# Word transposes of the probabilities, alternating with the score matmuls, in a two-problem attention kernel

## The chip, the cores and the metric

The kernel runs on one core of one Trainium2 chip. The metric is the time of one execution on the device in microseconds (us). Each figure for "the time" is the median of several executions. A profile of one further execution gives the starts and durations of the instructions on each engine: PE (TensorE matmuls; PEld is its weight load), DVE (VectorE), ACT (ScalarE), POOL (GpSimd) and SP (SyncE, which here only issues transfers).

## The reference

Two independent attention blocks, A and B, of the same sizes; their outputs stand side by side in the last dimension. In each, queries are projected from `x`, keys and values come from caches, and there is one softmax over 512 keys:

```python
B, Sq, D = 16, 144, 448
H, Sk, Dh = 16, 512, 256
q = (x @ wq).reshape(B, Sq, H, Dh).transpose(0, 2, 1, 3)
scores = jnp.einsum("bhqd,bhkd->bhqk", q, k_cache) * (Dh ** -0.5)
p = softmax(scores, axis=-1)
o = jnp.einsum("bhqk,bhkd->bhqd", p, v_cache)
out = o.transpose(0, 2, 1, 3).reshape(B, Sq, H * Dh) @ wo
...
return jnp.concatenate([a, b], axis=-1)
```

All inputs and outputs are bf16. Block B repeats its key heads by `Hq // Hkv`, which is 1.

## The kernel before

**Units.** A unit is one (block, batch, head): 2 x 16 x 16 = 512 units `U`. Four units make a group (one load of values, `t_load_v`, 1 MB), eight make a supergroup (one transposing load of keys, `t_load_k`). Of the 144 queries of a unit, the first 112 (`QA`) are worked on alone, and the last 32 (`QB`) of four units are put together into 128 rows. The first kind is called the 112-row part here, the second the 32-row part.

**The stages of a unit**, each with its engine:

- `t_q` (PE, L314): eight matmuls of 144 columns project the queries into the PSUM bank `qp_ps`; `t_evac_q` copies them to `qt_sb`, on DVE (L326) in four of eight iterations and on ACT (L330) in the others.
- `t_sa` (PE, L418): two matmuls of 512 columns, one for each half of the head's 256 dimensions, accumulate the scores of the 112-row part into one of two banks `sa_ps`, chosen by the unit's parity.
- `t_max` (DVE, L429), `t_exp` (ACT, L440, an activation and a read of its row sums), `t_recip` (DVE, L450) and `t_norm` (POOL, L458): the softmax. The probabilities stand in `pa_sb`, keys in the free dimension.
- `t_ta` (PE, L471): four transposes bring the keys to the partitions. Transpose `c` takes every fourth key, beginning at key `c`, so that partition `p` holds keys 4p to 4p+3, as the values are laid out. The result goes to the bf16 view `pta_ps` of the same bank `sa_ps`, chosen by parity again; `t_evac_pta` (DVE, L481) copies it to `pt_sb`.
- `t_pv` (PE, L504): eight matmuls of 144 columns with the values as weights, moving operand `pt_sb`; `t_evac_ot` (ACT, L519) copies the result to `ring`.
- `t_op_piece` (PE, L542): matmuls of 448 columns with `wo`, usually two for each iteration; more or none where chunks come due.

The 32-row part has the same stages for four units at once in the banks `sb_ps`: `t_sb` (L342, 16 matmuls for eight units), `t_max_b` (L354), `t_exp_b` (L364), `t_recip_b` (L374), `t_norm_b` (L382), `t_tb` (L394, four transposes of 128 columns) and `t_evac_ptb` (L403).

**Order.** One loop over `i` writes every engine's instruction list in program order. Iteration `i` handles Q of unit i+15 (`LQ`), scores, max and exp of unit i+5 (`LS`), reciprocal and normalisation of unit i+4, transposes of unit i+2 (`LT`) with their copy, and PV and its evacuation of unit i. On PE the order in an iteration is Q, SB (every eighth), SA, TA, TB (two in eight), PV, output matmuls. The queue SP issues the loads in an order planned by due times.

**Waits.** The class `_Sched` turns reads, writes and banks into semaphore waits, one wait for each engine, put ahead of the first instruction of an entry. An entry counts its engine's semaphore once, after its last instruction. The PSUM bank is a resource: an entry that touches a bank waits for the last use of that bank by another engine. Iteration `i` puts the scores of unit i+5 into one `sa_ps` bank; iteration i+1 puts the transposes of unit i+3 into the same bank, and iteration i+2 the scores of unit i+7. So each bank goes from scores (read by max and exp) to transposes (read by the copy) to scores again.

Of the kernel before, what the change touches and what calls it, by code (L numbers as in the profile page):

```python
# [5 lines left out]
BF16 = mybir.dt.bfloat16  # L6
F32 = mybir.dt.float32
# [115 lines left out]
def bass_concat_heads__mha_block_cached__gqa_block_cached__near_ridge_kernel(  # L123
# [19 lines left out]
    Bn, SQ, D = A_x.shape  # L143
    H, SK, DH = A_k_cache.shape[1], A_k_cache.shape[2], A_k_cache.shape[3]
    assert (SQ, D, SK, DH) == (144, 448, 512, 256), (SQ, D, SK, DH)
    assert H % 4 == 0
    QA, QB = 112, 32
    NU = Bn * H
    NT = NP * NU
# [11 lines left out]
    LQ, LS, LT = 15, 5, 2  # L161
# [3 lines left out]
    NQT, NPA, NPB, NPT, NST, NSTB, NOST = 12, 5, 2, 8, 4, 2, 3  # L165
# [9 lines left out]
    with contextlib.ExitStack() as es:  # L175
        def sb(name, shape, dt):
            return es.enter_context(nc.sbuf_tensor(name, shape, dt))

        def ps(name, shape, dt):
            return es.enter_context(nc.psum_tensor(name, shape, dt))  # L180
# [4 lines left out]
        kt_sb = sb("kt_sb", [128, NK, 2, 8 * SK], BF16)  # L185
        v_sb = sb("v_sb", [128, NV, 4, 4 * DH], BF16)
        xt_sb = sb("xt_sb", [128, NXG, 4, XB * SQ], BF16)
        qt_sb = sb("qt_sb", [128, NQT, 2, SQ], BF16)
        pa_sb = sb("pa_sb", [128, NPA, SK], BF16)
        pb_sb = sb("pb_sb", [128, NPB, SK], BF16)  # L190
        pt_sb = sb("pt_sb", [128, NPT, 4, SQ], BF16)
        ost_sb = sb("ost_sb", [128, NOST, D], BF16)
        ident = sb("ident", [128, 128], BF16)
        ones = sb("ones", [128, 128], BF16)
        stat = sb("stat", [128, 3 * NST + 3 * NSTB + 2], F32)
        qp_ps = ps("qp_ps", [128, 512], F32)
        sa_ps = [ps("sa_ps%d" % i, [128, 512], F32) for i in range(2)]
        sb_ps = [ps("sb_ps%d" % i, [128, 512], F32) for i in range(2)]
        ot_ps = [ps("ot_ps%d" % i, [128, 512], F32) for i in range(2)]
        op_ps = ps("op_ps", [128, 512], F32)  # L200
        pta_ps = [t.bitcast(BF16) for t in sa_ps]
        ptb_ps = [t.bitcast(BF16) for t in sb_ps]

        S = _Sched()
        sem_names = list(COMPUTE)
# [127 lines left out]
        def t_sb(SG):  # L333
            ksl = SG % NK

            def e(t):
                ins = None
                for dc in range(2):
                    for jj in range(8):
                        U = 8 * SG + jj  # L340
                        j = jj % 4
                        ins = t.matmul(sb_ps[jj // 4][32 * j:32 * j + 32, :], lhsT=qt_sb[:, U % NQT, dc, QA:SQ],  # L342
                                       rhs=kt_sb[:, ksl, dc, jj * SK:(jj + 1) * SK], start=(dc == 0), stop=(dc == 1),
                                       tile_position=(0, 32 * j))
                return ins
            S.add(PE, e, reads=[(("qt", (8 * SG + jj) % NQT), 8 * SG + jj) for jj in range(8)] + [(("kt", ksl), SG)],
                  writes=[(("sbb", 0), ("s", 2 * SG)), (("sbb", 1), ("s", 2 * SG + 1))], banks=["sb0", "sb1"],
                  name="SB%d" % SG)
# [38 lines left out]
        def t_tb(G):  # L387
            psl = G % NPB

            def e(t):  # L390
                src = pb_sb[:, psl, :].rearrange("q (p c) -> q c p", c=4)
                ins = None
                for c in range(4):
                    ins = t.transpose(ptb_ps[G % 2][:, c * 128:(c + 1) * 128], src[:, c, :], ident[:, :])  # L394
                return ins
            S.add(PE, e, reads=[(("pb", psl), (G, 1)), ("ident", 0)], writes=[(("sbb", G % 2), ("t", G))],
                  banks=["sb%d" % (G % 2)], name="TB%d" % G)

        def t_evac_ptb(G):
            s0 = (4 * G) % NPT  # L400

            def e(v):
                return v.tensor_copy(pt_sb[:, s0:s0 + 4, :, QA:SQ],  # L403
                                     ptb_ps[G % 2][:, 0:512].rearrange("p (c j q) -> p j c q", c=4, j=4))
            S.add(DVE, e, reads=[(("sbb", G % 2), ("t", G))],
                  writes=[(("ptb", (4 * G + j) % NPT), 4 * G + j) for j in range(4)], banks=["sb%d" % (G % 2)],
                  name="eptb%d" % G)

        def t_sa(U):
            SG = U // 8  # L410
            ksl = SG % NK
            bank = U % 2
            ko = (U % 8) * SK

            def e(t):
                ins = None
                for dc in range(2):
                    ins = t.matmul(sa_ps[bank][0:QA, :], lhsT=qt_sb[:, U % NQT, dc, 0:QA],  # L418
                                   rhs=kt_sb[:, ksl, dc, ko:ko + SK], start=(dc == 0), stop=(dc == 1))
                return ins  # L420
            S.add(PE, e, reads=[(("qt", U % NQT), U), (("kt", ksl), SG)], writes=[(("sap", bank), ("s", U))],
                  banks=["sa%d" % bank], name="SA%d" % U)

        def t_max(U):
            bank = U % 2
            sl = U % NST

            def e(v):
                return v.tensor_reduce(stat[0:QA, NEG + sl:NEG + sl + 1], sa_ps[bank][0:QA, :], axis=AX.X,  # L429
                                       op=ALU.max, negate=True)  # L430
            S.add(DVE, e, reads=[(("sap", bank), ("s", U))], writes=[(("neg", sl), U)], banks=["sa%d" % bank],
                  name="mx%d" % U)

        def t_exp(U):
            bank = U % 2
            sl = U % NST
            psl = U % NPA

            def e(a):
                return a.activation(pa_sb[0:QA, psl, :], sa_ps[bank][0:QA, :], AF.Exp,  # L440
                                    bias=stat[0:QA, NEG + sl:NEG + sl + 1], scale=1.0,
                                    accum_out=stat[0:QA, RSUM + sl:RSUM + sl + 1])
            S.add(ACT, e, reads=[(("sap", bank), ("s", U)), (("neg", sl), U)],
                  writes=[(("pa", psl), (U, 0)), (("rsum", sl), U)], banks=["sa%d" % bank], name="ex%d" % U)
# [15 lines left out]
            S.add(POOL, e, reads=[(("pa", psl), (U, 0)), (("rinv", sl), U)], writes=[(("pa", psl), (U, 1))],  # L460
                  name="nm%d" % U)

        def t_ta(U):
            psl = U % NPA
            bank = U % 2

            def e(t):
                src = pa_sb[0:QA, psl, :].rearrange("q (p c) -> q c p", c=4)
                ins = None
                for c in range(4):  # L470
                    ins = t.transpose(pta_ps[bank][:, c * 128:c * 128 + QA], src[:, c, :], ident[0:QA, 0:QA])  # L471
                return ins
            S.add(PE, e, reads=[(("pa", psl), (U, 1)), ("ident", 0)], writes=[(("sap", bank), ("t", U))],
                  banks=["sa%d" % bank], name="TA%d" % U)

        def t_evac_pta(U):
            sl = U % NPT
            bank = U % 2

            def e(v):  # L480
                return v.tensor_copy(pt_sb[:, sl, :, 0:QA],  # L481
                                     pta_ps[bank][:, 0:512].rearrange("p (c q) -> p c q", c=4)[:, :, 0:QA])
            S.add(DVE, e, reads=[(("sap", bank), ("t", U))], writes=[(("pta", sl), U)], banks=["sa%d" % bank],
                  name="epta%d" % U)

# [8 lines left out]
        def t_pv(U):  # L494
            G, j = divmod(U, 4)
            vsl = G % NV
            sl = U % NPT
            ob = U % 2

            def e(t):  # L500
                ins = None
                for dc in range(2):
                    for c in range(4):
                        ins = t.matmul(ot_ps[ob][:, dc * SQ:(dc + 1) * SQ],  # L504
                                       lhsT=v_sb[:, vsl, j, c * DH + dc * 128:c * DH + (dc + 1) * 128],
                                       rhs=pt_sb[:, sl, c, :], start=(c == 0), stop=(c == 3))
                return ins
            S.add(PE, e, reads=[(("v", vsl), G), (("pta", sl), U), (("ptb", sl), U)], writes=[(("otp", ob), U)],
                  banks=["ot%d" % ob], name="PV%d" % U)
# [75 lines left out]
        for XG in range(NXGT):  # L585
            pr, j = divmod(XG, Bn // XB)
# [64 lines left out]
        i = s_min  # L651
        while True:
# [21 lines left out]
            u = i + LQ  # L674
# [2 lines left out]
                t_evac_q(u)  # L677
            if do_sb and sgi > 0:
                t_sb(sgi)
            u = i + LS  # L680
            if 0 <= u < NT:
                t_sa(u)
                t_max(u)
                t_exp(u)
            u = i + LS - 1
            if 0 <= u < NT:
                t_recip(u)
                t_norm(u)
            u = i + LT
            if 0 <= u < NT:  # L690
                t_ta(u)
                t_evac_pta(u)
            if ok and ph == 3:
                t_tb(ga)
                t_evac_ptb(ga)
# [7 lines left out]
            u = i  # L703
# [97 lines left out]
```

## Time and profile before

| what | us |
|---|---|
| time, median of three runs (1212.93 to 1215.47) | 1213.23 |
| span of the profiled execution, first to last instruction | 1210.9 |
| PE busy with Q, L314, 4096 matmuls of 0.228 | 344.1 |
| PE busy with PV, L504, 4096 matmuls of 0.226 | 340.9 |
| PE busy with scores, L418, 1024 matmuls of 0.385 | 311.1 |
| PE busy with output matmuls, L542, 1120 of 0.353 | 279.6 |
| PE busy with transposes, L471, 2048 of 0.213 | 186.5 |

The span is 2.3 us under the median; the time also has what lies around the first and last instruction. Matmuls of PE overlap: the next one starts while the last drains, so a matmul's duration is longer than its share of the time, and the times in the table add up to more than the span. What a matmul costs in a row of matmuls is read from the distance between starts. The granted TensorE clock of the profiled execution was 0.997 of full speed.

In a line of the page's table of groups stand the code line, the engine, the operation, the tiles (out<-in), shapes and count; then, after the first bar, the time in which the group was busy and the mean duration of one instruction in ns; after the second, how long the engine was idle just before them and who ended most of that idle time. A line of the timeline has the start (us from the start of the span), the duration of the whole run of like instructions, the engine and line, the shapes, and in brackets the idle time before it with its releaser. A line of the tile view has the shortest, median and longest duration in ns.

### The profile page before, as it was taken

What the parts mean: (1) busy time and instruction counts of PE and PEld (TensorE: products, weight loads), DVE (VectorE), ACT (ScalarE), POOL (GpSimd) and SP (SyncE); (2) the same over time, 40 slices, a digit from 0 to 9 for tenths busy, and PEclk for the clock granted to TensorE, in tenths of its full rate; (3) what the DMA queues carried; (4) which work ended last, traced back from release to release, by engine and by line L of the source; (5) the groups of instructions that cost most, each with busy time, mean ns of one, the idle gap of its engine ahead of it and who ended that gap; (6) DMA issues with size and microseconds to landing.
All of it is one profiled execution on the core that took longest, in us unless ns stands there. A gap on an engine that the chain in (4) does not pass through costs nothing.

```text
span 1210.9 us, 33868 instructions
## 1 busy us (share of the span) xinstructions
PE 1176.6 (97%) x13952; PEld 902.6 (75%) x13952; DVE 770.1 (64%) x2179; ACT 753.9 (62%) x2213; POOL 679.6 (56%) x682
## 2 busy tenths in 40 slices
PE   4998999999999999999999999999999999999997
PEld 3676777777777777777777777777877777777765
DVE  1765666666666666666566666666666666666563
ACT  1655666666666666666566666666666666666553
POOL 0654565565555565565555655655655655655553
PEclk9999999999999999999999999999999999999999
DMA  9999999999999999999999999999999999999971
GB/s 250 296 269 290 246 255 225 242 251 246 245 238 234 228 263 231 239 239 233 278 284 272 278 272 267 247 257 224 245 245 236 226 245 244 244 239 243 223 178 47
DMA packets 627033, 294.15 MB, mean 243 GB/s; under 512 B 548416, under 2 KB 556608, under 8 KB 626880
## 3 DMA queue, kind: packets, MB, share of 16 engines
q1 hardware_dynamic: 625152, 287.85, 102.2%
q0 software_dynamic: 1728, 4.13, 1.2%
q8 instruction: 111, 1.82, 0.6%
q14 instruction: 42, 0.34, 0.1%
HBM read 148.90 MB, written 4.13 MB: 126 GB/s over the span
## 4 chain that ended last, share of the span: by engine, by line
PE 90%; DMA 6%; DVE 2%; SPq 1%; ACT 0%; issue 0%; POOL 0%; ACTq 0%
PE qp_ps L314 20%; PE ot_ps L504 19%; PE sa_ps L418 18%; PE op_ps L542 17%; PE sa_ps L471 8%; PE sb_ps L342 5%; DMA kt_sb<-in_A_k_cache_dram 4%; PE sb_ps L394 2%; DMA kt_sb<-in_B_k_cache_dram 1%; DVE stat L429 1%; DMA wq_sb<-in_A_wq_dram 0%; PE qp_ps L542 0%; SPq L280 0%; DVE qt_sb L326 0%; DVE pt_sb L481 0%
## 5 line engine op out<-in xcount | busy, mean ns | idle before, releaser
L458 POOL TENSOR_TENSOR pa_sb<-pa_sb,stat 112x512 bf16<-112x512 bf16 x512 | 532.7, 1041 | 491.6 <-DVE stat L450 491.4
L440 ACT ACTIVATE pa_sb<-sa_ps,stat 112x512 bf16<-112x512 f32 x512 | 352.0, 688 | 409.6 <-DVE stat L429 408.6
L429 DVE TENSOR_REDUCE stat<-sa_ps 112x1 f32<-112x512 f32 x512 | 353.9, 691 | 324.7 <-PE sa_ps L418 321.4
L314 PEld LDWEIGHTS qp_ps<-xt_sb,wq_sb 128*128 128x128 bf16 x4096 | 290.5, 99 | 93.1 <-issue 11.3
L314 PE MATMUL qp_ps<-xt_sb,wq_sb 128*128 128x144 bf16 x4096 | 344.1, 228 | 16.1 <-DMA wq_sb<-in_A_wq_dram 10.3
L504 PE MATMUL ot_ps<-pt_sb,v_sb 128*128 128x144 bf16 x4096 | 340.9, 226 | 0.0
L418 PE MATMUL sa_ps<-kt_sb,qt_sb 128*112 128x512 bf16 x1024 | 311.1, 385 | 1.0 <-DVE pt_sb L481 0.8
L542 PE MATMUL op_ps<-wo_sb,ring 128*128 128x448 bf16 x1120 | 279.6, 353 | 0.0
L504 PEld LDWEIGHTS ot_ps<-pt_sb,v_sb 128*128 128x128 bf16 x4096 | 269.1, 98 | 0.4
L471 PEld LDWEIGHTS sa_ps<-ident,pa_sb 112*128 112x128 bf16 x2048 | 161.2, 114 | 104.9 <-ACT pa_sb L440 24.8
L519 ACT ACTIVATE ring<-ot_ps 128x288 bf16<-128x288 f32 (+8 forms) x512 | 190.3, 372 | 4.5 <-PE ot_ps L504 4.5
L481 DVE COPY pt_sb<-sa_ps 128x448 bf16<-128x448 bf16 x512 | 190.5, 372 | 2.4 <-PE sa_ps L471 2.4
L471 PE MATMUL sa_ps<-ident,pa_sb 112*128 112x112 bf16 x2048 | 186.5, 213 | 0.1
L326 DVE TENSOR_SCALAR qt_sb<-qp_ps 128x288 bf16<-128x288 f32 x256 | 117.0, 457 | 98.2 <-PE qp_ps L314 97.5
L382 POOL TENSOR_TENSOR pb_sb<-pb_sb,stat 128x512 bf16<-128x512 bf16 x128 | 133.1, 1040 | 27.1 <-DVE stat L374 27.1
L330 ACT ACTIVATE qt_sb<-qp_ps 128x288 bf16<-128x288 f32 x256 | 106.0, 414 | 35.1 <-PE qp_ps L314 33.4
L418 PEld LDWEIGHTS sa_ps<-kt_sb,qt_sb 128*112 128x112 bf16 x1024 | 96.9, 129 | 38.5 <-issue 26.8
L542 PEld LDWEIGHTS op_ps<-wo_sb,ring 128*128 128x128 bf16 x1120 | 95.5, 98 | 28.1 <-issue 0.9
L440 ACT ACTIVATION_READ_ACCUMULATOR pa_sb<-sa_ps,stat 112x1 f32 x512 | 98.9, 193 | 0.0
L354 DVE TENSOR_REDUCE stat<-sb_ps 128x1 f32<-128x512 f32 x128 | 87.1, 680 | 3.6 <-PE sb_ps L342 3.6
L364 ACT ACTIVATE pb_sb<-sb_ps,stat 128x512 bf16<-128x512 f32 x128 | 88.5, 691 | 0.0
L450 DVE RECIPROCAL stat<-stat 112x1 f32<-112x1 f32 x512 | 78.4, 153 | 0.5 <-ACT pa_sb L440 0.5
(23 smaller groups left out, 368.4 us busy)
## 6 DMA issues: line engine op xcount, KB each, us to landing
v_sb<-in_A_v_cache_dram SPq DMA_DIRECT2D x64, 1024.0 KB, 6.0
v_sb<-in_B_v_cache_dram SPq DMA_DIRECT2D x64, 1024.0 KB, 6.1
out_dram<-ost_sb POOLq DMA_DIRECT2D x36, 112.0 KB, 5.1
wo_sb<-in_A_wo_dram SPq DMA_DIRECT2D x8, 448.0 KB, 7.4
wo_sb<-in_B_wo_dram SPq DMA_DIRECT2D x8, 448.0 KB, 5.7
wq_sb<-in_A_wq_dram SPq DMA_DIRECT2D x4, 768.0 KB, 6.2
wq_sb<-in_B_wq_dram SPq DMA_DIRECT2D x4, 768.0 KB, 7.8
wq_sb<-in_A_wq_dram SPq DMA_DIRECT2D x4, 128.0 KB, 6.6
```

Source lines behind the costliest of these rows:

```text
L314: ins = t.matmul(qp_ps[:, dc * SQ:(dc + 1) * SQ], lhsT=wq_sb[:, kc, c0:c0 + 128], rhs=xt_sb[:, xsl, kc, xo:xo + SQ], start=(kc == 0 and dc ...
L326: return v.tensor_scalar(qt_sb[:, sl, :, :], src, 1.0 / 16.0, None, op0=ALU.mult)
L382: return g.tensor_tensor(pb_sb[:, psl, :], pb_sb[:, psl, :], stat[:, RINVB + sl:RINVB + sl + 1].to_broadcast([128, SK]), op=ALU.mult)
L418: ins = t.matmul(sa_ps[bank][0:QA, :], lhsT=qt_sb[:, U % NQT, dc, 0:QA], rhs=kt_sb[:, ksl, dc, ko:ko + SK], start=(dc == 0), stop=(dc == 1))
L429: return v.tensor_reduce(stat[0:QA, NEG + sl:NEG + sl + 1], sa_ps[bank][0:QA, :], axis=AX.X, op=ALU.max, negate=True)
L440: return a.activation(pa_sb[0:QA, psl, :], sa_ps[bank][0:QA, :], AF.Exp, bias=stat[0:QA, NEG + sl:NEG + sl + 1], scale=1.0, accum_out=stat ...
L458: return g.tensor_tensor(pa_sb[0:QA, psl, :], pa_sb[0:QA, psl, :], stat[0:QA, RINV + sl:RINV + sl + 1].to_broadcast([QA, SK]), op=ALU.mult)
L471: ins = t.transpose(pta_ps[bank][:, c * 128:c * 128 + QA], src[:, c, :], ident[0:QA, 0:QA])
L481: return v.tensor_copy(pt_sb[:, sl, :, 0:QA], pta_ps[bank][:, 0:512].rearrange("p (c q) -> p c q", c=4)[:, :, 0:QA])
L504: ins = t.matmul(ot_ps[ob][:, dc * SQ:(dc + 1) * SQ], lhsT=v_sb[:, vsl, j, c * DH + dc * 128:c * DH + (dc + 1) * 128], rhs=pt_sb[:, sl, c, ...
L519: ins = a.activation(ring[:, 2 * h:2 * h + 2, c0:c0 + n1], src[:, :, 0:n1], AF.Copy)
L542: ins = t.matmul(acc[0:m, 0:D], lhsT=ring[:, c, col0:col0 + m], rhs=wo_sb[:, c, :], start=(c == first), stop=(c == last))
```

## The change

A probability is 2 bytes; two neighbouring keys make a 4-byte word. After the change the transposes move words: `pa_sb` and `pb_sb` are viewed as F32 (`pa_w`, `pb_w`), a transpose `c` takes every second word, and two transposes bring over what four did. The identity is F32. `pt_sb` keeps the two keys of a word side by side for each query, so PV's moving operand takes every second bf16 element. The copies go from bf16 views (`pta_h`, `ptb_h`) of the banks to `pt_sb`.

The entries `t_sa` and `t_ta` become one entry for each matmul and each transpose, and the loop writes them alternately: first score matmul of unit i+5, first transpose of unit i+2, second score matmul, second transpose. The max and the exp of unit i+5 are written after these; the order on DVE, ACT, POOL and SP stays as it was. In the 32-row part the two word transposes stand together, in the old place.

```diff
-        pt_sb = sb("pt_sb", [128, NPT, 4, SQ], BF16)
+        pt_sb = sb("pt_sb", [128, NPT, 2, SQ, 2], BF16)
...
-        ident = sb("ident", [128, 128], BF16)
-        ones = sb("ones", [128, 128], BF16)
+        ident = sb("ident", [128, 128], F32)
+        ones = sb("ones", [128, 128], F32)
...
-        pta_ps = [t.bitcast(BF16) for t in sa_ps]
-        ptb_ps = [t.bitcast(BF16) for t in sb_ps]
+        pta_ps = sa_ps
+        ptb_ps = sb_ps
+        pta_h = [t.bitcast(BF16) for t in sa_ps]
+        ptb_h = [t.bitcast(BF16) for t in sb_ps]
+        pa_w = pa_sb.bitcast(F32)
+        pb_w = pb_sb.bitcast(F32)
...
-                src = pb_sb[:, psl, :].rearrange("q (p c) -> q c p", c=4)
+                src = pb_w[:, psl, :].rearrange("q (p c) -> q c p", c=2)
                 ins = None
-                for c in range(4):
+                for c in range(2):
                     ins = t.transpose(ptb_ps[G % 2][:, c * 128:(c + 1) * 128], src[:, c, :], ident[:, :])
...
-                return v.tensor_copy(pt_sb[:, s0:s0 + 4, :, QA:SQ],
-                                     ptb_ps[G % 2][:, 0:512].rearrange("p (c j q) -> p j c q", c=4, j=4))
+                return v.tensor_copy(pt_sb[:, s0:s0 + 4, :, QA:SQ, :].rearrange("p j c q e -> p j c (q e)"),
+                                     ptb_h[G % 2][:, 0:512].rearrange("p (c j q) -> p j c q", c=2, j=4))
...
-        def t_sa(U):
+        def t_sa(U, dc):
...
-                ins = None
-                for dc in range(2):
-                    ins = t.matmul(sa_ps[bank][0:QA, :], lhsT=qt_sb[:, U % NQT, dc, 0:QA],
-                                   rhs=kt_sb[:, ksl, dc, ko:ko + SK], start=(dc == 0), stop=(dc == 1))
-                return ins
+                return t.matmul(sa_ps[bank][0:QA, :], lhsT=qt_sb[:, U % NQT, dc, 0:QA],
+                                rhs=kt_sb[:, ksl, dc, ko:ko + SK], start=(dc == 0), stop=(dc == 1))
...
-        def t_ta(U):
+        def t_ta(U, c):
...
-                src = pa_sb[0:QA, psl, :].rearrange("q (p c) -> q c p", c=4)
-                ins = None
-                for c in range(4):
-                    ins = t.transpose(pta_ps[bank][:, c * 128:c * 128 + QA], src[:, c, :], ident[0:QA, 0:QA])
-                return ins
+                src = pa_w[0:QA, psl, :].rearrange("q (p c) -> q c p", c=2)
+                return t.transpose(pta_ps[bank][:, c * 128:c * 128 + QA], src[:, c, :], ident[0:QA, 0:QA])
...
-                return v.tensor_copy(pt_sb[:, sl, :, 0:QA],
-                                     pta_ps[bank][:, 0:512].rearrange("p (c q) -> p c q", c=4)[:, :, 0:QA])
+                return v.tensor_copy(pt_sb[:, sl, :, 0:QA, :].rearrange("p c q e -> p c (q e)"),
+                                     pta_h[bank][:, 0:512].rearrange("p (c q) -> p c q", c=2)[:, :, 0:2 * QA])
...
-                                       rhs=pt_sb[:, sl, c, :], start=(c == 0), stop=(c == 3))
+                                       rhs=pt_sb[:, sl, c // 2, :, c % 2], start=(c == 0), stop=(c == 3))
...
-            u = i + LS
-            if 0 <= u < NT:
-                t_sa(u)
-                t_max(u)
-                t_exp(u)
+            us, ut = i + LS, i + LT
+            for half in range(2):
+                if 0 <= us < NT:
+                    t_sa(us, half)
+                if 0 <= ut < NT:
+                    t_ta(ut, half)
+            if 0 <= us < NT:
+                t_max(us)
+                t_exp(us)
...
-            u = i + LT
-            if 0 <= u < NT:
-                t_ta(u)
-                t_evac_pta(u)
+            if 0 <= ut < NT:
+                t_evac_pta(ut)
```

In the prediction SA.0, SA.1, TA.0 and TA.1 are the first and second score matmul and the first and second transpose of an iteration.

More of the change, by code (lines that the diff above doesn't have):

```diff
@@ L415, in e @@
             def e(t):
-                ins = None
-                for dc in range(2):
-                    ins = t.matmul(sa_ps[bank][0:QA, :], lhsT=qt_sb[:, U % NQT, dc, 0:QA],
-                                   rhs=kt_sb[:, ksl, dc, ko:ko + SK], start=(dc == 0), stop=(dc == 1))
-                return ins
+                return t.matmul(sa_ps[bank][0:QA, :], lhsT=qt_sb[:, U % NQT, dc, 0:QA],
+                                rhs=kt_sb[:, ksl, dc, ko:ko + SK], start=(dc == 0), stop=(dc == 1))
             S.add(PE, e, reads=[(("qt", U % NQT), U), (("kt", ksl), SG)], writes=[(("sap", bank), ("s", U))],
-                  banks=["sa%d" % bank], name="SA%d" % U)
+                  banks=["sa%d" % bank], name="SA%d.%d" % (U, dc))
         def t_max(U):
@@ L467, in e @@
             def e(t):
-                src = pa_sb[0:QA, psl, :].rearrange("q (p c) -> q c p", c=4)
-                ins = None
-                for c in range(4):
-                    ins = t.transpose(pta_ps[bank][:, c * 128:c * 128 + QA], src[:, c, :], ident[0:QA, 0:QA])
-                return ins
+                src = pa_w[0:QA, psl, :].rearrange("q (p c) -> q c p", c=2)
+                return t.transpose(pta_ps[bank][:, c * 128:c * 128 + QA], src[:, c, :], ident[0:QA, 0:QA])
             S.add(PE, e, reads=[(("pa", psl), (U, 1)), ("ident", 0)], writes=[(("sap", bank), ("t", U))],
-                  banks=["sa%d" % bank], name="TA%d" % U)
+                  banks=["sa%d" % bank], name="TA%d.%d" % (U, c))
         def t_evac_pta(U):
```

## The prediction

> **What bounds the kernel now.** I read the page's busy times first, then the waits, then the timeline of single units (a unit is one batch and head). Times are us where no unit stands. The page:
>
> ```profile
> span 1210.9 us, 33868 instructions
> PE 1176.6 (97%) x13952; PEld 902.6 (75%) x13952; DVE 770.1 (64%) x2179; ACT 753.9 (62%) x2213; POOL 679.6 (56%) x682
> ...
> L440 ACT ACTIVATE pa_sb<-sa_ps,stat 112x512 bf16<-112x512 f32 x512 | 352.0, 688 | 409.6 <-DVE stat L429 408.6
> L429 DVE TENSOR_REDUCE stat<-sa_ps 112x1 f32<-112x512 f32 x512 | 353.9, 691 | 324.7 <-PE sa_ps L418 321.4
> ...
> L504 PEld LDWEIGHTS ot_ps<-pt_sb,v_sb 128*128 128x128 bf16 x4096 | 269.1, 98 | 0.4
> L471 PEld LDWEIGHTS sa_ps<-ident,pa_sb 112*128 112x128 bf16 x2048 | 161.2, 114 | 104.9 <-ACT pa_sb L440 24.8
> ```
>
> PE is the bound, so shorter PE work ought to pay. But PE waits inside a unit must be checked first. This is the timeline of an ordinary unit:
>
> ```profile
> 601.56 0.59 PE L418 MATMUL sa_ps<-kt_sb,qt_sb 128*112 128x512 bf16 x2
> ...
> 602.00 0.36 PE L471 MATMUL sa_ps<-ident,pa_sb 112*128 112x112 bf16 x4
> ...
> 602.19 0.67 PE L504 MATMUL ot_ps<-pt_sb,v_sb 128*128 128x144 bf16 x8
> 602.20 0.69 DVE L429 TENSOR_REDUCE stat<-sa_ps 112x1 f32<-112x512 f32 x1
> ...
> 602.70 0.54 PE L542 MATMUL op_ps<-wo_sb,ring 128*128 128x448 bf16 x2
> ...
> 602.92 0.69 ACT L440 ACTIVATE pa_sb<-sa_ps,stat 112x512 bf16<-112x512 f32 x1 [0.93 <-DVE stat L429]
> ...
> 603.07 0.66 PE L314 MATMUL qp_ps<-xt_sb,wq_sb 128*128 128x144 bf16 x8
> 603.51 0.19 ACT L440 ACTIVATION_READ_ACCUMULATOR pa_sb<-sa_ps,stat 112x1 f32 x1
> ...
> 603.57 0.59 PE L418 MATMUL sa_ps<-kt_sb,qt_sb 128*112 128x512 bf16 x2
> ```
>
> Differences of starts give the stream times: two scores 0.43, four transposes 0.19 (0.047 each, 112 columns), PV 0.51, two output matmuls 0.37, Q 0.50; the unit takes 2.01. Read the softmax beside it: the max ends 602.89, exp and its accumulator end 603.70, just before the next transposes. Those write the bank that this exp reads (banks alternate by unit parity: scores of i+5, then transposes of i+3). So the transposes of one iteration wait for the exp of the iteration before. A stretch without output matmuls shows that wait ending last:
>
> ```profile
> 324.18 0.69 DVE L429 TENSOR_REDUCE stat<-sa_ps 112x1 f32<-112x512 f32 x1
> ...
> 325.29 0.64 PE L418 MATMUL sa_ps<-kt_sb,qt_sb 128*112 128x512 bf16 x2
> ...
> 325.50 0.19 ACT L440 ACTIVATION_READ_ACCUMULATOR pa_sb<-sa_ps,stat 112x1 f32 x1
> ...
> 325.74 0.24 PEld L471 LDWEIGHTS sa_ps<-ident,pa_sb 112*128 112x128 bf16 x4 [0.28 <-ACT pa_sb L440]
> ```
>
> The weight load starts 0.05 after the accumulator read ends (325.69). The max starts 0.04 after the second score matmul's record (0.38) ends: 325.29+0.64=325.93 against 325.96. So from the start of the second score matmul to the release of the next iteration's transposes: 0.38+0.04+1.51 (324.18 to 325.69)+0.05=1.98; finer starts over 84 such places give **1.972**.
>
> **The change part by part.**
>
> *Fewer transposes.* Two per unit instead of four and, at L394, two instead of four per four units. If a word streams like a bf16 key, a unit saves 2x0.047=0.094 and each of 128 TBs about 0.10 of its 0.22. The trace has no 4-byte matmul. Bounds: 0.047 each (nearest row, L471, same columns), or four times that, 0.19. I take 0.047; the half-speed and four-fold cases are rivals.
>
> The Trainium skill speaks on both sides: "FP8 and Floating Point Precision", TensorE Precision Notes, gives true FP32 four passes; "TensorE: Matmul & The Clock Gate", Terms, calls transpose mode four times faster for FP32. No row here decides; by the first rule the sum would be that of the four-fold rival, by the second that of my value.
>
> *Weight loads.* These rows of the tile view give the price by columns:
>
> ```profile
> L342 PEld LDWEIGHTS sb_ps<-kt_sb,qt_sb x1024: 92/97/151, 23.7 to 1170.3; 128*32 128x32 bf16 x171
> L418 PEld LDWEIGHTS sa_ps<-kt_sb,qt_sb x1024: 126/130/130, 28.8 to 1194.3; 128*112 128x112 bf16 x171
> ```
>
> 80 more columns cost 33 ns, 0.41 each. A 128-column load escapes this at L504 (98 ns). For words I take the slow rate, 128x0.41=0.053 exposed where nothing covers it, bounds 0.026 (the spacing of L471's first two loads where they had waited) and 0.107 (twice 0.053). In the new order each word load has a 0.21 score matmul before it as cover, except where its wait ends last.
>
> *The new order.* SA.0, TA.0, SA.1, TA.1. Nothing on DVE, ACT, POOL or SP is reordered, but TA.0 carries the wait for the previous iteration's exp, and SA.1 is now queued behind it on PE. DVE's max waits for SA.1, the exp for the max, the next TA.0 for the exp: a loop of **one** iteration, whereas before both scores went ahead of the wait. A unit's interval cannot be under 1.972 + word load 0.053 + TA.0 0.047 + what remains of SA.1's load (112 columns, 0.046, under a 0.047 stream: 0 to 0.05, I take 0.02) = **2.09**, bounds 2.05 and 2.15. An ordinary unit's PE work alone would fall to 1.92. So TA.0 would wait: from SA.1's start PE reaches TA.0 after 0.21+0.05+0.51+0.37+0.50+0.21=1.85, but the release comes at 1.972. What is late next is SA.1, with it the max; the loop keeps it so.
>
> The 511 intervals between successive second score matmuls, by starts in the timeline: 72 of mean 1.77 (no output matmul), 17 of 1.906, 224 of 2.012, 45 of 2.237 (nearly all with a TB), 153 of mean 2.97 (score blocks of the 32-row part, more output matmuls, DMA waits). With floor 2.09:
> 72x0.32=+23.0; 17x0.184=+3.1; 224x0.078=+17.5; 45x(2.09-2.237)=-6.6; 153x-0.094=-14.4; TB in 64 of the long ones, -0.10 each=-6.4. Sum **+16.2**. Each 0.01 of floor is worth 313 to 355 intervals, about 3.4 us; the balance lies at 2.045.
>
> *Other edits.* At two iterations in eight L354's max (0.68) follows the copy on DVE and L326's evacuation (0.46) comes next, ahead of the loop's max: 1.47+0.68+0.46=2.61 after SA.1's start against 2.09+0.42=2.51 wanted. Bounds 0 and 128x0.10=13; I take +5. Copies L481 (0.37) and L403 move the same bytes in longer runs: 0; L481's own loop, 0.42+0.68+0.37+0.06+0.05+0.21+0.05=1.84, is covered by 2.09. The identity in f32 is two POOL instructions at the start, under the first 10.3 us wait for wq: 0, or under 1 if uncovered. PV now reads pt_sb at a step of two. L471's load at a step of four takes 114 against 98 at L504, so bounds 0 and 15 ns x8=0.12 per unit; short units cover it (2.09-1.92=0.17), the 153 long ones would pay 18. I take 0, as moving rows here run at column rate. No DMA issue moves; V loads on SP wait for PE already (235 us behind L542), so they follow. The places where PE waits for kt_sb (7.9+0.8 us) absorb part of what is lost ahead of them: 0 to -9, I take -4.
>
> *Sum.* +16+5-4=+17 on the profiled span 1210.9, which is 2.3 below the 1213.23 median of the runs; with the same 2.3 around it, **1230**. Own range: floor 2.05 to 2.15 (+2 to +37), DVE 0 to 13, PV 0 to 18, absorption to -9, TB gain absent +11 (most of it under the floor): 1214 to 1262.
>
> **Rivals.**
>
> *Faster: the exp is not what TA.0 waits for.* Then PE streams: 512x0.094+128x0.10=61 less, of which some 11 stay with the short units held by L481's loop at 1.84: 1163. For: PE busy 97%, the waits view charges only 24.8 us to this exp, DVE and ACT are under 65% busy. Against: the load in the ordinary unit starts only 0.04 after the release (603.79 against 603.70+0.05). It decides from a floor below 2.045, which needs load, stream and remainder within 0.07; at a floor of 2.00 it gives 1199.
>
> *Half speed.* Word loads 0.107, streams 0.094: no stream gained, floor 1.972+0.107+0.094=2.17. 72x0.40+17x0.26+224x0.16=69, less 45x0.07=3: about +66, 1279. For: twice the bytes per column. Against: no row shows bytes, rather than columns, set the pace.
>
> *Four-fold.* Each word transpose 0.19: a unit +0.19, TB +0.21, floor 1.972+0.053+0.19=2.215: 72x0.45+17x0.31+224x0.20+45x0.40+153x0.19+64x0.21=+143, 1356, and up to 1410 if each pass loads again.
>
> **How the numbers follow.** Forecast 0.56; half speed 0.14; four-fold 0.13; faster 0.12; balance within 0.2% 0.05 (0.2%, 2.4 us, is about what this kernel's runs can tell from no change). The likeliest's time is 1230. The range runs from 1198, which takes in a floor of 2.00 and some two fifths of the faster case, to 1300, above half speed: left out are 0.13 above and 0.07 below. Faster 0.12, same 0.05, slower 0.83.
>
> **What would show it.** In the timeline after: a load of L471 (its new line) idle before it with the exp as releaser in most units; ordinary intervals at 2.07 to 2.13 instead of 2.01, and the 1.78 ones gone; ACT's wait for L429 and PE idle time up, DVE and ACT busy sums unchanged. Wrong if ordinary intervals are near 1.92 (no loop), if two word transposes take more than 0.12 where nothing waits (speed), or if PV's eight take over 0.51.

## The result, and the profile after

The change makes the kernel **slower**: 1284.72 us median of four runs (1284.00 to 1285.32) against 1214.29 (1212.93 to 1215.47) of the kernel before on the same chip; ratio 1.058, interval 1.0564 to 1.0596. The profiled span went from 1210.9 to 1282.3, 71.4 more. The forecast was slower, by 17: the direction was right, and the loss is four times the one forecast. The granted clock of the profiled execution was 0.999, against 0.997 before, so the loss is not the clock's. Times are in us below where no unit stands.

The page after, with the lines that answer to those of before:

```profile
span 1282.3 us, 31308 instructions
PE 1248.4 (97%) x12672; PEld 987.7 (77%) x12672; DVE 775.4 (60%) x2179; ACT 748.7 (58%) x2213; POOL 679.3 (53%) x682
...
L441 ACT ACTIVATE pa_sb<-sa_ps,stat 112x512 bf16<-112x512 f32 x512 | 351.8, 687 | 488.9 <-DVE stat L430 488.7
L430 DVE TENSOR_REDUCE stat<-sa_ps 112x1 f32<-112x512 f32 x512 | 354.2, 692 | 404.6 <-PE sa_ps L420 402.6
...
L470 PE MATMUL sa_ps<-ident,pa_sb 112*128 112x112 f32 x1024 | 300.8, 294 | 2.6 <-ACT pa_sb L441 0.2
...
L470 PEld LDWEIGHTS sa_ps<-ident,pa_sb 112*128 112x128 f32 x1024 | 202.6, 198 | 72.4 <-ACT pa_sb L441 71.9
```

DVE and ACT do the same work for as long as before (ACT's exp 351.8 against 352.0), but each waits 80 longer: ACT for the max, the max for the scores. PE has 1024 transposes in the 112-row part instead of 2048 and still shows 97% busy; "busy" includes matmuls whose record is open while the next instruction waits (below, the first score matmul is on record from 645.16 to 645.54, while the load after it waits until 645.43). So PE's idle time, which the prediction wanted up, stayed at 34. The last line names the wait: the loads of the word transposes stood 71.9 behind the exp, against 24.8 before. One such load takes 198 ns on average, against 114.

Two stretches of the timeline show it. First an iteration in which nothing waits for the exp, then, 2 us later, one in which the first transpose does:

```profile
643.36 0.26 PE L470 MATMUL sa_ps<-ident,pa_sb 112*128 112x112 f32 x1
...
643.46 0.38 PE L420 MATMUL sa_ps<-kt_sb,qt_sb 128*112 128x512 bf16 x1
...
643.67 0.26 PE L470 MATMUL sa_ps<-ident,pa_sb 112*128 112x112 f32 x1
...
643.77 0.68 PE L502 MATMUL ot_ps<-pt_sb,v_sb 128*128 128x144 bf16 x8
643.87 0.69 DVE L430 TENSOR_REDUCE stat<-sa_ps 112x1 f32<-112x512 f32 x1 [4.47 <-PE sa_ps L420]
...
644.60 0.69 ACT L441 ACTIVATE pa_sb<-sa_ps,stat 112x512 bf16<-112x512 f32 x1 [4.42 <-DVE stat L430]
...
645.16 0.38 PE L420 MATMUL sa_ps<-kt_sb,qt_sb 128*112 128x512 bf16 x1
645.18 0.19 ACT L441 ACTIVATION_READ_ACCUMULATOR pa_sb<-sa_ps,stat 112x1 f32 x1
...
645.43 0.19 PEld L470 LDWEIGHTS sa_ps<-ident,pa_sb 112*128 112x128 f32 x1 [0.19 <-ACT pa_sb L441]
...
645.64 0.38 PE L420 MATMUL sa_ps<-kt_sb,qt_sb 128*112 128x512 bf16 x1
```

In the first, a word transpose holds PE for 0.10 (643.36 to 643.46 and 643.67 to 643.77): two words cost 0.20, what four bf16 transposes cost. In the second, the accumulator read ends at 645.37, the load starts 0.06 later, and only 0.21 after that the second score matmul starts. The whole chain stands in these lines: second score matmul (643.46), max (643.87), exp (644.60), accumulator read (645.18), load of the next iteration's first transpose (645.43), which is 1.97 in all, and then that iteration's second score matmul (645.64). In 356 of 509 iterations the load starts within 60 ns of the accumulator read's end, against 87 before.

The starts of the second score matmul give an interval for each unit. Sorted by what each interval was before:

| interval before, count, mean | mean after | sum of differences |
|---|---|---|
| under 1.85, 72, 1.770 | 2.164 | +28.4 |
| 1.85 to 1.99, 17, 1.906 | 2.186 | +4.8 |
| 1.99 to 2.13, 224, 2.012 | 2.184 | +38.7 |
| 2.13 to 2.30, 45, 2.237 | 2.281 | +2.0 |
| over 2.30, 153, 2.969 | 2.953 | -2.5 |

Unrounded, the sum is 71.3, all but 0.1 of the difference of the spans. 311 of the 511 intervals are 2.18 or 2.19 after the change: a floor, not a spread.

### The profile page after: what moved, and what is told of

Same layout as the page of the kernel before. It is cut to its first block, busy times and chain, and to the rows that moved or that the text cites. A ratio compares the mean times of both kernels' runs of the same rounds, so it can differ in the third digit from the quotient of the medians.

```text
span 1282.3 us, 31308 instructions
## 1 busy us (share of the span) xinstructions
PE 1248.4 (97%) x12672; PEld 987.7 (77%) x12672; DVE 775.4 (60%) x2179; ACT 748.7 (58%) x2213; POOL 679.3 (53%) x682
## 4 chain that ended last, share of the span: by engine, by line
PE 94%; DVE 2%; DMA 2%; issue 1%; SPq 0%; ACT 0%; POOL 0%; ACTq 0%
PE ot_ps L502 20%; PE qp_ps L318 19%; PE sa_ps L420 19%; PE op_ps L540 16%; PE sa_ps L470 12%; PE sb_ps L346 5%; PE sb_ps L398 2%; DMA kt_sb<-in_B_k_cache_dram 2%; DVE stat L430 1%; DMA wq_sb<-in_A_wq_dram 0%; DVE pt_sb L407 0%; DVE pt_sb L479 0%; PE qp_ps L540 0%; DVE qt_sb L330 0%; ACT qt_sb L334 0%
## 5 line engine op out<-in xcount | busy, mean ns | idle before, releaser
L441 ACT ACTIVATE pa_sb<-sa_ps,stat 112x512 bf16<-112x512 f32 x512 | 351.8, 687 | 488.9 <-DVE stat L430 488.7
L420 PE MATMUL sa_ps<-kt_sb,qt_sb 128*112 128x512 bf16 x1024 | 381.9, 386 | 2.8 <-DVE pt_sb L479 1.1
L502 PE MATMUL ot_ps<-pt_sb,v_sb 128*128 128x144 bf16 x4096 | 348.4, 226 | 0.0
L502 PEld LDWEIGHTS ot_ps<-pt_sb,v_sb 128*128 128x128 bf16 x4096 | 300.2, 97 | 10.6
L470 PE MATMUL sa_ps<-ident,pa_sb 112*128 112x112 f32 x1024 | 300.8, 294 | 2.6 <-ACT pa_sb L441 0.2
L470 PEld LDWEIGHTS sa_ps<-ident,pa_sb 112*128 112x128 f32 x1024 | 202.6, 198 | 72.4 <-ACT pa_sb L441 71.9
L420 PEld LDWEIGHTS sa_ps<-kt_sb,qt_sb 128*112 128x112 bf16 x1024 | 167.9, 164 | 48.7 <-issue 26.8
```

The lines of the kernel that those rows point to most:

```text
L420: return t.matmul(sa_ps[bank][0:QA, :], lhsT=qt_sb[:, U % NQT, dc, 0:QA], rhs=kt_sb[:, ksl, dc, ko:ko + SK], start=(dc == 0), stop=(dc == 1))
L470: return t.transpose(pta_ps[bank][:, c * 128:c * 128 + QA], src[:, c, :], ident[0:QA, 0:QA])
L502: ins = t.matmul(ot_ps[ob][:, dc * SQ:(dc + 1) * SQ], lhsT=v_sb[:, vsl, j, c * DH + dc * 128:c * DH + (dc + 1) * 128], rhs=pt_sb[:, sl, c ...
```

## The experiments

All ratios are to the kernel before on the same chip.

**Words in the old order.** Only the loop is put back:

```diff
             for half in range(2):
                 if 0 <= us < NT:
                     t_sa(us, half)
+            for half in range(2):
                 if 0 <= ut < NT:
                     t_ta(ut, half)
```

> The words stay, the order goes back: both score matmuls, then both word transposes. Loop theory (the loss comes from TA.0's wait for the exp standing ahead of SA.1): the 2.18 us floor goes; ordinary intervals between second score matmuls 2.03 to 2.05 (2.01 before, plus 0.017 for the pair of words and 0.017 for PV's strided operand), short ones 1.78 again, time 1225 to 1236. Rival (the words themselves cost it, as loads and streams at half speed on PE, in any order): about as after the change, 1275 to 1290, ordinary intervals over 2.15.

Measured 1231.14, ratio 1.0143 (1.0128 to 1.0158). The timeline of an ordinary unit:

```profile
656.20 0.59 PE L420 MATMUL sa_ps<-kt_sb,qt_sb 128*112 128x512 bf16 x2
...
656.42 0.41 PEld L470 LDWEIGHTS sa_ps<-ident,pa_sb 112*128 112x128 f32 x2
...
656.63 0.38 PE L470 MATMUL sa_ps<-ident,pa_sb 112*128 112x112 f32 x2
...
656.85 0.36 PE L502 MATMUL ot_ps<-pt_sb,v_sb 128*128 128x144 bf16 x3
```

And the line of the waits view for the transposes' loads (total, times, longest):

```profile
PEld sa_ps L470 <- ACT pa_sb L441: 23.3, 87, 0.5
```

In the timeline the loads have no bracket, so they do not wait, and in the whole run their wait for the exp is back at what it was before (23.3 against 24.8); the two words take 0.22 (656.63 to 656.85) against 0.19 to 0.20 for four bf16 transposes. 221 intervals are 2.04 or 2.05 and 69 are 1.78 again; the floor is gone. So 17 of the 70 lost come with the words in the old order (PV's strided reading and the split entries included), and 53 only with the new order.

**The order alone, with bf16 transposes.** The kernel before, with `t_sa` and `t_ta` cut in two and written alternately, two transposes ahead of the second score matmul or one:

```diff
-                t_sa(u)
...
-                t_ta(u)
...
+            us, ut = i + LS, i + LT
+            for half, cs in enumerate((range(0, 2), range(2, 4))):
+                if 0 <= us < NT:
+                    t_sa(us, half)
+                if 0 <= ut < NT:
+                    t_ta(ut, cs)
```

(In the other run `range(0, 1), range(1, 4)`.)

> The kernel before with the order alone changed: first score matmul, two bf16 transposes, second score matmul, two bf16 transposes. Loop theory: floor 1.972 + first load 0.03 + two streams about 0.10 = 2.10, 313 intervals lifted to it, time 1250 to 1265. Rival (words cost it): 1211 to 1217.

> As the run with two transposes first, but one transpose ahead of the second score matmul and three behind. Loop theory: floor lower by one stream, 2.05, time 1236 to 1250, some 16 us under the run with two first. Rival (words cost it): 1211 to 1217, no difference between the two.

Measured 1252.98, ratio 1.0331 (1.0314 to 1.0348) with two first, and 1239.35, ratio 1.0213 (1.0197 to 1.0228) with one first. Both are as expected; between them lie 13.6, where some 16 were expected. The instructions are those of the kernel before; only PE's order differs, and the entries are split, as they also are in the run with words in the old order, where that and the words together cost 17. From the waits view and the timeline of the run with two first, then from the timeline of the run with one first:

```profile
PEld sa_ps L468 <- ACT pa_sb L437: 75.3, 312, 0.7
```

```profile
652.76 0.19 ACT L437 ACTIVATION_READ_ACCUMULATOR pa_sb<-sa_ps,stat 112x1 f32 x1
...
653.01 0.15 PEld L468 LDWEIGHTS sa_ps<-ident,pa_sb 112*128 112x128 bf16 x2 [0.20 <-ACT pa_sb L437]
...
653.14 0.38 PE L416 MATMUL sa_ps<-kt_sb,qt_sb 128*112 128x512 bf16 x1
```

```profile
651.74 0.19 ACT L437 ACTIVATION_READ_ACCUMULATOR pa_sb<-sa_ps,stat 112x1 f32 x1
...
651.99 0.11 PEld L468 LDWEIGHTS sa_ps<-ident,pa_sb 112*128 112x128 bf16 x1 [0.16 <-ACT pa_sb L437]
...
652.07 0.38 PE L416 MATMUL sa_ps<-kt_sb,qt_sb 128*112 128x512 bf16 x1
```

The same wait, as often (312 times) as after the change. What differs is the distance from the load's start to the second score matmul: 0.131 with two transposes (653.01 to 653.14), 0.082 with one (651.99 to 652.07), 0.211 with one word. The interval of the units that are held follows it: 2.104, 2.055 and 2.185 (medians). In all three the rest is **1.973** within 0.001, the time from a second score matmul through max and exp to the start of the next first load. So whatever stands between the release and the second score matmul is paid once in each unit that is held. The rival (order without effect) is out.

**Words from neighbouring places.** Each word transpose of the 112-row part takes 128 neighbouring words instead of every second one. Probabilities then meet other keys' values, and the 112-row part's output differs.

```diff
-                src = pa_w[0:QA, psl, :].rearrange("q (p c) -> q c p", c=2)
+                src = pa_w[0:QA, psl, :].rearrange("q (c p) -> q c p", c=2)
```

> As after the change, but the two word transposes of the 112-row part take 128 neighbouring words each instead of every second one, so probabilities meet other keys' values and that part of the output differs. Tells why the word load takes 195 ns: if by the 4-byte width, loads stay at 195 ns, floor 2.18, time 1282 to 1288. If by the step of two words, loads fall to some 140 ns, floor 2.13, time 1255 to 1270.

Measured 1268.87, ratio 1.0457 (1.0441 to 1.0472). The tile view, shortest, median and longest in ns; first after the change, then this run:

```profile
L470 PEld LDWEIGHTS sa_ps<-ident,pa_sb x1024: 194/196/224, 33.8 to 1270.8; 112*128 112x128 f32 x171
L470 PE MATMUL sa_ps<-ident,pa_sb x1024: 259/261/375, 33.8 to 1270.9; 112*128 112x112 f32 x171
```

```profile
L470 PEld LDWEIGHTS sa_ps<-ident,pa_sb x1024: 137/142/272, 34.1 to 1255.5; 112*128 112x128 f32 x171
L470 PE MATMUL sa_ps<-ident,pa_sb x1024: 257/261/394, 34.1 to 1255.6; 112*128 112x112 f32 x171
```

The load falls from 196 to 142, so the step of two words costs it 54 ns. The 142 lie close to the 137 that the bf16 loads of 32 and 112 columns (97 and 130) would give at 128, if they went on at the same rate. But the bf16 loads that do have 128 columns are shorter: 98 from neighbouring places (PV before) and 113 at a step of four (the transposes before). So against the load that it replaces the word load is 83 longer, 54 of it by its own step; the other 29 came with the change from bf16 at a step of four to neighbouring words, and no run takes these apart further. The floor falls by about as much as the load, to 2.127, with 0.155 from load to score matmul. The transpose itself is as long as before, so its 0.100 is not the step's doing.

**Two things in the kernel before.** The table of intervals showed 72 short ones, most of 1.78, where PE has only 1.63 of work (no output matmuls: 2.01-0.38). In the kernel before, 72 intervals are of 1.80 or less. Three runs try to win that back without the change: the reciprocal written after the transposes' copy; the output matmuls spread out; both.

```diff
-            u = i + LS - 1
-            if 0 <= u < NT:
-                t_recip(u)
-                t_norm(u)
...
                 t_evac_pta(u)
+            u = i + LS - 1
+            if 0 <= u < NT:
+                t_recip(u)
+                t_norm(u)
...
-                credit += OP_RATE
+                credit += 2.0 if len(fifo["op"]) <= 40 else 2.5
+            if i < u_tail0 - 14:
+                credit = min(credit, 3.0)
```

> The kernel before with one thing moved on DVE: the reciprocal of unit i+4 (and its normalisation on POOL) is written after the copy of the transposes instead of ahead of it. If the 72 short intervals of 1.78 are held by DVE's chain max, reciprocal, copy to the next score matmul, they fall to some 1.71 and the time by 4 to 6, to about 1209. Rival (short intervals are held by something else, or the later normalisation holds the transposes back): 1212 to 1217 or more.

> The kernel before with the output matmuls spread more evenly: two in an iteration, four now and then, instead of ten at once and then iterations without any. If an interval without output matmuls loses 0.15 to DVE's chain, some 50 of these fewer give 6 to 9 less, 1205 to 1208. Rival (PE's total work sets the time, wherever the output matmuls stand): 1212 to 1216.

> Both together. If both act on the same intervals, the sum is less than the parts: some 1204 to 1207. Rival: 1212 to 1217.

| kernel | median | ratio, interval | intervals of 1.80 or less |
|---|---|---|---|
| reciprocal after copy | 1212.91 | 0.9979 (0.9967 to 0.9990) | 71, most now 1.72 |
| spread out | 1209.29 | 0.9948 (0.9932 to 0.9964) | 42, most 1.78 |
| both | 1208.79 | 0.9946 (0.9930 to 0.9962) | 42, most 1.72 |

The reciprocal: the short intervals fell by 0.06 as the DVE chain asks, 3.6 in the profile, but the long intervals of that execution gave 3.0 back, most at places that are long before too (1.2 and 1.5 early, 3.4 at the change from A to B); which wait ends last there stays open. Of the 4 to 6 expected, some 2 came out, and the time lies in the rival's range, although the short intervals did fall. Spreading: 5.6 of the expected 6 to 9, with 30 short intervals fewer instead of 50. Neither this nor both together reached the time expected (1205 to 1208 and 1204 to 1207). Both together differ from spreading alone by less than the intervals. These two are the best versions seen, half a per cent under the kernel before.

## Why the prediction was right and wrong

**Right: the loop.** The forecast said that TA.0 would wait for the previous iteration's exp, with SA.1 queued behind it, and that this makes a floor of 1.972 plus what lies between release and SA.1. The first part has a median of 1.973 or 1.974 in all four kernels with the new order (after the change, the two with bf16, the one with neighbouring words), and the order alone, without words, loses 3.3%. That ordinary intervals would be one even number and the 1.78 ones gone came true.

**Wrong: the size of two terms in that sum.** The step that failed is "If a word streams like a bf16 key", with "I take 0.047", and beside it "For words I take the slow rate, 128x0.41=0.053". A word streams 112 columns in 0.100, not 0.047. What is exposed of the strided load, with what remains of SA.1's load, is 0.211-0.100=0.111, not 0.053+0.02; the traces don't part the two. Load, stream and remainder, taken as 0.12, are 0.211: the floor is 2.184 instead of 2.09. The prediction's own sign for this, two word transposes over 0.12 where nothing waits, came with 0.20. In the 313 intervals that were under the floor this makes +71.8 instead of +43.6, 28 of the missing 54. The stream's other use in the sum, 0.094 saved in every unit that is not held, came to 0: the 153 long intervals stand at -2.5, and at +4.6 without the six in which the waits for keys moved (below), instead of -20.8 (two TB words start 0.13 apart, so two take about 0.25 against 0.22 for four bf16 transposes), and the 45 near 2.24 at +2.0 instead of -6.6, above the floor instead of on it.

The forecast chose the bf16 row because it had the same columns. It was nearest in shape, but not in type, and the type was what the change altered. The half-speed rival had both terms nearly right: load 0.107 and stream 0.094 gave 1279, and the measured time is 1284.7. It was given a chance of only 0.14, although no row of the trace bore on the speed of 4-byte words.

**Smaller terms.** DVE's late max, taken at +5: nothing; the max starts 0.417 to 0.420 after SA.1's start in 98 of 100 units (0.415 to 0.417 in 95 of 100 before). PV's strided operand, taken at 0: eight matmuls' starts span 0.454 instead of 0.439, some 0.017 a unit, hidden under the floor and paid only in the long ones. Waits for keys, taken at -4: the five intervals that shrank most by them gave back 9.2, one grew by 2.0; in the waits view PE's waits for the keys fell from 8.7 to 2.4. The copies of the 112-row part cost what they did (372 ns both times).

**The rules weighed there.** Of the two, neither fits the measured price. The Trainium skill's "FP8 and Floating Point Precision", TensorE Precision Notes, has four passes for true FP32; "TensorE: Matmul & The Clock Gate", Terms, has transpose mode four times faster for FP32. Here a column of words costs 0.100/112=0.89 ns, a column of bf16 0.049/112=0.44: twice.

A third page bears on the load: the Trainium skill's "SBUF — State Buffer", in its section on the DMA port swizzle, has full bandwidth for reads that hit the same 16-byte line at least twice, and gives four FP32 elements as how far one can stride for free. A step of two words, two reads in a line, is within that. The run with neighbouring words shows otherwise for a weight load: this step costs 54 ns of 196.

**Open.** That a word streams at half the speed of a bf16 column is measured, not explained: whether the 0.100 is set by reading the f32 identity, by the words in the array or by the f32 write to PSUM was not tried.

## What to carry to other kernels

Before two dependent streams on one engine are interleaved in its program order, write down for each wait what then stands behind it: here a wait that had been last in its group came to stand before an instruction that feeds its own next release, and a loop of two iterations became one. Its period is the chain plus every nanosecond between release and that instruction, and it shows in the timeline as one repeated interval. A row of another element type is no evidence for the price of the type that a change brings in, and halving the instructions gains nothing if each then takes twice as long.

## What the runs showed of the hardware

A transpose of 4-byte words takes 0.100 for 112 columns, twice the 0.049 of bf16, so moving two keys in a word is no gain in PE time. A 128-column weight load of words takes 142 ns from neighbouring places and 196 at a step of two words; of bf16, 98 from neighbouring places and 113 at a step of four. A matmul's moving operand at a step of two bf16 elements costs some 2 ns more for 144 columns (0.454 against 0.439 over seven distances).
